# Attention scores and reads of a batch in one call each, by heads of one parity

## The chip, the cores and the metric

The kernel runs on 1 core of one Trainium2 chip. The metric is device time in microseconds of one execution. Its engines are TensorE (PE in the profile, with PEld for its weight loads), VectorE (DVE), ScalarE (ACT), GpSimd (POOL) and SyncE (SP, which issues all DMAs here). They have a queue each and meet only through semaphores.

## The reference, cut to what matters

Attention between x, 8 batches of 8 heads of 512 tokens of 64 values, and a state of 32 rows of 64 values a head, in both directions; then two gated feed-forward layers.

```python
B, H, S, D = x.shape                      # 8, 8, 512, 64; state has Ns = 32 rows a head
scale = 1.0 / np.sqrt(D)
scores = scale * np.matmul(x, state.transpose(0, 1, 3, 2))
scores = scores - scores.max(-1, keepdims=True)
a = np.exp(scores)
a /= a.sum(-1, keepdims=True) + 1e-09
xread = np.matmul(a, state)
scores2 = scale * np.matmul(state, x.transpose(0, 1, 3, 2))
...
sread = np.matmul(a2, x)                  # a2: softmax of scores2 over the tokens
...
x = x @ w_a * (x @ w_b) @ w_out           # first layer, on the 4096 + 256 rows
x = silu(x @ w_gate) * (x @ w_val) @ w_out   # second layer
```

## The kernel before, in words

A block is the 512 tokens of a batch; a ninth block, "s", holds the 256 rows of sread. The first layer runs in steps of f, 128 of the 1536 hidden columns: two products `p` (line 644) into two PSUM banks, their elementwise product `a`, a split of it into a high and a low part `hs`, and four products `po` (line 679) with the output weights. A product is three matmuls, high by high, high by low and low by high, 0.227 us each. The first layer's input weights are first multiplied with the states (`sw`, lines 452 and 453, from `state_w`), so that xread itself is never made: the weights `a` of the attention go straight into the products `p` as `xs`. `sw` is copied out of PSUM (`swo`), goes to DRAM, and comes back as `swr`, split into `swh` and `swl`; that of the first step goes straight into `swr`, eight DMAs of 32 rows. The second layer (from about 710 us on) is made of other lines and isn't touched.

The attention of a batch is two quads g of four heads each. `quad` (lines 483 to 517) loads two pairs of heads of x, transposed (`xt`, 64 values of the even head over 64 of the odd one, 512 tokens). Two matmuls make the scores `psc` (line 493): the weights are a pair's states, 64 columns with zeros where a head doesn't meet its own values, so that a pair fills 64 of the bank's 128 partitions. Batches 0 and 1 (`BY_ROWS`) also make scores with the tokens on the partitions, `pr` (line 509), eight matmuls a quad whose weights are 128 tokens of x. `softmax1` turns scores into `xs`; `softmax2` takes the softmax over the tokens, turns it by four transpositions (`pa`), reads `psr` with x by tokens (`xn`, line 607: eight matmuls of 64 columns of weights and 128 moved columns, half of them a head's values by the other head's weights), scales the result (`sr`, line 613), transposes it (`pst`, line 618) and keeps its valid halves by two copies into `sread` (line 628). All this is in float32, where one matmul of the code is two records in the trace.

The order of the work on each engine is written out by a planner, `Program.order`: it keeps a list of tasks with a due time (`by`), an earliest time (`start`), estimated costs, and numbers of buffers (`ROOM`), and hands each free engine the most urgent task. Copies go to ACT or DVE as it finds them free. Only the order reaches the chip. Two PSUM banks, "pt", serve the scores from batch 1 on, the transpositions, the reads and `sw`. Until the first product, spare matmuls `warm` (line 1043) fill PE.

Of the kernel before, what the change touches and what calls it, by code (L numbers as in the profile page):

```python
# [14 lines left out]
AF = mybir.ActivationFunctionType  # L15
# [3 lines left out]
P = 128  # L19
B, H, S, NS, D = 8, 8, 512, 32, 64  # L20
# [4 lines left out]
NPAIR = H // 2  # L25
# [42 lines left out]
PASS_US, HALF_PASS_US = 0.2267, 0.12  # L68
SWITCH_US = 0.2
# [6 lines left out]
def act(n):  # L76
    return {"ACT": ACT_US[0] + ACT_US[1] * n}
# [181 lines left out]
class Kernel:  # L259
# [183 lines left out]
    def state_w(self, st, fp, p, w, q, by):  # L443

        hi, lo = st
        for h in range(2):
            head = 2 * p + h
            c = slice(head * P, (head + 1) * P)
            ps = self.bank(f"sw{q}_{fp}_{head}")

            def fn(pe, ps=ps, h=h, c=c):
                pe.matmul(ps.t, lhsT=hi.t[:, c], rhs=w.t[:, h], start=True, stop=False)  # L452
                pe.matmul(ps.t, lhsT=lo.t[:, c], rhs=w.t[:, h], start=False, stop=True)  # L453

            self.pe(2 * PASS_US, fn, [hi, lo, (w, (h, 0)), (w, (h, 1))], [ps], by=by)
            r = 32 * (head % 4)
            self.sw_out(
                ps, self.sw_d[q, fp], lambda t, head=head, r=r: t[:, head // 4, r:r + 32].rearrange("b n c -> n b c"), f"swo{q}_{fp}_{head}", by,
                (self.sw_first, head) if q == fp == 0 else None
            )  # L460

# [13 lines left out]

    def attention(self, b, start, span, by_x, by_s):

        raw_st = self.load(
            self.h_buf(f"strt{b}"), self.st_t[b], P * 1024, lambda t: t[:, :NPAIR * 2 * NS], start=start
        )  # L480
        return [self.quad(b, g, start + span * g / 2, span, raw_st, by_x, by_s) for g in range(2)]

    def quad(self, b, g, t0, span, raw_st, by_x, by_s):

        nm = f"{b}_{g}"
        x = [self.load(self.h_buf(f"xt{nm}_{j}"), self.xt[b, 2 * g + j], start=t0) for j in range(2)]
        sT = self.h_buf(f"sT{nm}")
        ps = self.bank(f"psc{nm}", g if b == 0 else None)
        cols = [slice((2 * g + j) * 64, (2 * g + j + 1) * 64) for j in range(2)]

        def fn(pe):
            for j in range(2):
                pe.matmul(
                    ps.t[64 * j:64 * j + 64], lhsT=raw_st.t[:, cols[j]], rhs=x[j].t, start=True, stop=True
                )

        due = t0 + span * 0.15 if b >= BY_ROWS else by_s - 60
        self.pe(4 * PASS_US + SWITCH_US, fn, [raw_st, *x], [ps], by=due)
        self.copy(lambda: sT.t, lambda: ps.t, 512, [ps], [sT], by=due + 2)
        if b >= BY_ROWS:  # L500
            x_hl = self.softmax1(b, g, sT, by_x)
        else:
            pr = self.ring(f"ab{g}", 1, f"pr{nm}", self.ps) if b == 0 else self.bank(f"pr{nm}")

            def by_rows(pe):
                for c in range(4):
                    r = slice(c * P, (c + 1) * P)
                    for j in range(2):
# [59 lines left out]
    def softmax2(self, b, g, sT, by):  # L568

        nc = self.nc  # L570
        nm = f"{b}_{g}"
        e2 = self.h_buf(f"e2{nm}")
        st = self.ring("s2", 4, f"s2{nm}", shape=(4,))
        kw = {"by": by}

        def first(v):
# [5 lines left out]
            out=e2.t, in_=sT.t, func=AF.Exp, scale=SCALE, bias=st.t[:, 1:2], accum_out=st.t[:, 2:3]  # L582
# [17 lines left out]
        ps = self.bank(f"psr{nm}")  # L600

        def fn(pe):
            for c in range(4):
                for j in range(2):
                    l = slice(c * P + 64 * j, c * P + 64 * j + 64)
                    r = slice(c * 256 + P * j, c * 256 + P * j + P)
                    pe.matmul(  # L607
                        ps.t[64 * j:64 * j + 64, :P], lhsT=a2.t[:, l], rhs=xn.t[:, r], start=c == 0, stop=c == 3
                    )

        self.pe(0.9 + SWITCH_US, fn, [a2, xn], [ps], **kw)
        sr = self.h_buf(f"sr{nm}")
        self.p.add(act(P), lambda e: nc.scalar.activation(
            out=sr.t[:, :P], in_=ps.t[:, :P], func=AF.Copy, scale=st.t[:, 3:4]
        ), [ps, st], [sr], **kw)
        pt = self.bank(f"pst{nm}")
# [4 lines left out]
        for h in range(2):  # L621
            rows = slice(64 * h, 64 * h + 64)

            def kept(rows=rows, h=h):
                return pt.t[rows, :P].rearrange("p (j i n) -> p j i n", j=2, n=NS)[:, :, h]

            self.copy(
                lambda rows=rows: self.sread.t[rows, 2 * g:2 * g + 2, b::B], kept, 64, [pt],
                [(self.sread, (b, g, h))], **kw
            )  # L630
# [534 lines left out]
def laid_out(inputs):  # L1165
    x, state = inputs["x"], inputs["state"]
    arrays = {}
    arrays["xt"] = x.transpose(0, 1, 3, 2).reshape(B, NPAIR, P, S)
    arrays["xn"] = x.reshape(B, 2, 4, 4, P, D).transpose(0, 1, 4, 3, 2, 5).reshape(B, 2, P, 1024)

    sp = state.reshape(B, NPAIR, 2, NS, D)
    st_t = np.zeros((B, 2, D, NPAIR, 2, NS), state.dtype)
    for h in range(2):
        st_t[:, h, :, :, h] = sp[:, :, h].transpose(0, 3, 1, 2)
    arrays["st_t"] = st_t.reshape(B, P, NPAIR * 2 * NS)
# [38 lines left out]
```

## Time and profile before

| | |
|---|---|
| median of 3 runs | 1460.92 us (1459.82 to 1461.51) |
| the profiled execution | 1460.34 us, of which its span 1458.6 |
| PE, DVE, ACT busy | 1441.6, 1026.4, 717.4 us |
| mean granted clock | 0.998 |
| matmul records of scores, reads, scores by rows | 64, 256, 64 |
| DMA | 344.73 MB, 236 GB/s |

The span is that from the first to the last instruction. A busy PE is not one at its peak: records overlap, and the time that a group takes of PE is read from where the next group starts. A granted clock of 1 is 2.4 GHz, one of 0.5 is 1.2 GHz. Idle time of an engine that nobody waits for costs nothing.

### The profile page before, as it was taken

The page shows a single profiled execution, that of the slowest core. Times are in us where ns is not written, and L with a number is a line of the kernel's source. Part 1 is how long each engine was busy: PE and PEld are TensorE (multiplying, and loading weights), DVE is VectorE, ACT ScalarE, POOL GpSimd, SP SyncE. Part 2 cuts the span into 40 slices and gives each one's busy share as a digit, 9 for nine tenths or more (in the row PEclk, how much of TensorE's full clock was granted, in tenths as well). Part 3 has the DMA queues.
Part 4 walks back from the last instruction along what each step waited for, and adds up shares of the span by engine and source line. Part 5 has one row for each costly group of instructions (what it writes and reads, how often), then busy time and mean ns, then how long its engine had stood idle before and what let it go on. Part 6 is the DMA issues. An engine that isn't in the chain of part 4 may idle for free.

```text
span 1458.6 us, 19824 instructions
## 1 busy us (share of the span) xinstructions
PE 1441.6 (99%) x6968; PEld 1189.5 (82%) x6968; DVE 1026.4 (70%) x1750; ACT 717.4 (49%) x1276; POOL 103.7 (7%) x78
## 2 busy tenths in 40 slices
PE   9999899999999999999999999999999999999998
PEld 8677688778888888998888888888888888888887
DVE  7899756875778788877687796655955567554464
ACT  7676745753456465655554553333523354323340
POOL 1202201110011111111010100000000000000000
PEclk9999999999999999999999999999999999999999
DMA  8765754762467575856989796675947668365476
GB/s 300 260 244 177 259 174 145 245 228 80 162 217 258 178 263 217 289 205 221 347 316 329 255 358 264 228 257 174 366 169 269 209 233 320 139 246 204 143 263 242
DMA packets 134420, 344.73 MB, mean 236 GB/s; under 512 B 14000, under 2 KB 16048, under 8 KB 134320
## 3 DMA queue, kind: packets, MB, share of 16 engines
q1 hardware_dynamic: 134320, 343.46, 66.4%
q8 instruction: 55, 0.90, 0.3%
q14 instruction: 45, 0.37, 0.1%
HBM read 246.94 MB, written 95.94 MB: 235 GB/s over the span
## 4 chain that ended last, share of the span: by engine, by line
PE 84%; DMA 3%; DVE 2%; ACT 1%; issue 0%; SPq 0%; DVEq 0%; ACTq 0%
PE pX L772 17%; PE pu L931 15%; PE po L679 15%; PE p L644 14%; PE pC L772 8%; PE pY L772 4%; PE p_s L644 2%; PE po_s L679 1%; PE pvs L644 1%; PE pgs L644 1%; PE pus L986 1%; PE sw L452 1%; DMA swr<-sw 1%; PE psr L607 1%; DMA wt<-wt 1%; PE sw L453 1%
## 5 line engine op out<-in xcount | busy, mean ns | idle before, releaser
L679 PE MATMUL po<-hs,wo 128*128 128x512 f32 x1152 | 287.4, 392 | 0.8 <-DVE hs L338 0.4
L679 PEld LDWEIGHTS po<-hs,wo 128*128 128x128 f32 x1152 | 213.9, 188 | 53.4 <-issue 7.3
L931 PE MATMUL pu<-S,wt 128*128 128x512 f32 x1008 | 242.8, 389 | 0.0
L644 PE MATMUL p<-xs,swh 128*128 128x512 f32 x768 | 239.7, 394 | 1.9 <-DVE a L663 1.2
L931 PEld LDWEIGHTS pu<-S,wt 128*128 128x128 f32 x1008 | 188.9, 188 | 39.0
L772 PE MATMUL pX<-x,w 128*128 128x512 f32 x864 | 219.6, 390 | 0.3 <-ACT t L330 0.3
L772 PEld LDWEIGHTS pX<-x,w 128*128 128x128 f32 x864 | 161.9, 188 | 34.6 <-ACT t L330 1.2
L644 PEld LDWEIGHTS p<-xs,swh 128*128 128x128 f32 x768 | 143.6, 189 | 35.4 <-DVE a L663 2.5
L644 PE MATMUL p<-xs,swl 128*128 128x512 f32 x384 | 150.3, 392 | 0.4 <-DVE swl L338 0.4
L780 DVE TENSOR_TENSOR t<-t,pC 128x512 f32<-128x512 f32 x96 | 65.9, 687 | 106.5 <-ACT t L330 94.3
L663 DVE TENSOR_TENSOR a<-a,p 128x512 f32<-128x512 f32 x96 | 65.8, 685 | 75.6 <-PE p L644 60.3
L330 ACT COPY a<-p 128x512 f32<-128x512 f32 x86 | 50.4, 586 | 98.4 <-PE p L644 97.3
L330 ACT COPY t<-pX 128x512 f32<-128x512 f32 x83 | 48.7, 586 | 99.0 <-PE pX L772 95.1
L345 ACT CAST hs<-a 128x512 fp32r<-128x512 f32 x96 | 59.5, 621 | 68.6 <-DVE a L663 56.1
L644 PEld LDWEIGHTS p<-xs,swl 128*128 128x128 f32 x384 | 72.5, 189 | 16.7 <-DVE swl L338 1.3
L338 DVE TENSOR_TENSOR hs<-a,hs 128x512 fp32r<-128x512 f32 x96 | 67.5, 704 | 14.7 <-ACT hs L345 14.2
L772 PE MATMUL pX<-x,wg 128*128 128x512 f32 x288 | 73.2, 390 | 0.0
L772 PE MATMUL pY<-x,wg 128*128 128x512 f32 x288 | 73.1, 389 | 0.0
L772 PE MATMUL pC<-x,wv 128*128 128x512 f32 x288 | 73.1, 389 | 0.0
L772 PE MATMUL pC<-x,w 128*128 128x512 f32 x288 | 73.1, 389 | 0.0
L338 DVE TENSOR_TENSOR swl<-swr,swh 128x1024 fp32r<-128x1024 f32 x48 | 59.8, 1246 | 11.0 <-ACT swh L345 6.4
L786 ACT ACTIVATE gv<-pX 128x512 f32<-128x512 f32 x48 | 28.7, 598 | 74.2 <-PE pX L772 74.2
(181 smaller groups left out, 2214.1 us busy)
## 6 DMA issues: line engine op xcount, KB each, us to landing
w<-w SPq DMA_DIRECT2D x120, 512.0 KB, 5.7
wt<-wt SPq DMA_DIRECT2D x84, 512.0 KB, 6.6
sw<-swo SPq DMA_DIRECT2D x96, 256.0 KB, 3.2
wg<-w2g SPq DMA_DIRECT2D x48, 512.0 KB, 5.6
swr<-sw SPq DMA_DIRECT2D x47, 512.0 KB, 5.1
raw_w<-in_wab SPq DMA_DIRECT2D x24, 512.0 KB, 6.3
wv<-w2v SPq DMA_DIRECT2D x36, 256.0 KB, 6.9
xt<-in_xt SPq DMA_DIRECT2D x32, 256.0 KB, 5.1
```

The source lines that it names most:

```text
L330: self.nc.scalar.copy(out(), in_())
L338: lambda e: self.by_engine[e].tensor_tensor(out=out(), in0=in0(), in1=in1(), op=ALU.subtract), r, w, **kw
L345: self.p.add(act(n), lambda e: self.nc.scalar.copy(hi(), src()), [src_buf], [hb], **kw)
L452: pe.matmul(ps.t, lhsT=hi.t[:, c], rhs=w.t[:, h], start=True, stop=False)
L453: pe.matmul(ps.t, lhsT=lo.t[:, c], rhs=w.t[:, h], start=False, stop=True)
L644: pe.matmul(ps.t[:, :n], lhsT=l, rhs=r, start=i == 0, stop=i == last)
L663: self.vec(n, lambda v, a=a, pb=pb: v.tensor_tensor(out=a.t[:, :n], in0=a.t[:, :n], in1=pb.t[:, :n], op=ALU.mult), [pb], [a])
L679: pe.matmul(ps.t[:, :n], lhsT=wo[f].t[:, hw, c], rhs=hs.t[:, hh, :n], start=st, stop=sp)
L772: pe.matmul(ps.t, lhsT=w.t[:, half, hw, i * P:(i + 1) * P], rhs=x.t[:, hx], start=start and i == n == 0, stop=stop and i == 1 and n == 2, ...
L780: self.vec(512, lambda e: e.tensor_tensor(out=to(), in0=a(), in1=b(), op=op), r, [w], **kw)
L786: self.p.add(act(n), lambda e: self.nc.scalar.activation(out=out.t[:, :n], in_=ps.t[:, :n], func=AF.Silu), [ps], [out])
L931: pe.matmul(ps.t, lhsT=w.t[:, half, hw, c], rhs=x.t[:, hx], start=starts and k == m == 0, stop=stops and k == n - 1 and m == 2, skip_group ...
```

## The change

Heads are now grouped by parity: bank and softmax h hold the four heads 2j + h of a batch, j from 0 to 3, and the quads are gone. The layout of the states loses its zeros (32 columns a pair), `xn` and the rows of `sw` in DRAM are put in the new order of heads, with DMAs of the same sizes. Scores are one call a batch, eight matmuls with tiles of 64 rows by 32 columns of weights, into two banks. Scores by rows are 32 matmuls a batch of 64x128 tiles and 32 moved columns. The reads are one call a batch, 32 matmuls of 128x32 tiles and 64 moved columns into one bank, with no part left unused; its scaling is two ACT instructions of 64 columns, its transposition one for two, and the copy into `sread` one for four. All four loads of a batch's x have one earliest time, for batches 0 and 1 halfway to their block (`X_LATER`).

```diff
+X_LATER = 0.5
...
-            r = 32 * (head % 4)
+            r = 32 * (head // 2)
...
-                lambda: raw.t[r:r + 32, head // 4], lambda: o.t[::4], [o], [(raw, head)], 32 * 2048, by=by + 3
+                lambda: raw.t[r:r + 32, head % 2], lambda: o.t[::4], [o], [(raw, head)], 32 * 2048, by=by + 3
...
-        return [self.quad(b, g, start + span * g / 2, span, raw_st, by_x, by_s) for g in range(2)]
...
-        x = [self.load(self.h_buf(f"xt{nm}_{j}"), self.xt[b, 2 * g + j], start=t0) for j in range(2)]
...
+        n = NPAIR * NS
+        raw_st = self.load(self.h_buf(f"strt{b}"), self.st_t[b], P * 4 * n, lambda t: t[:, :n], start=start)
+        t0 = start + span * X_LATER if b < BY_ROWS else start
+        xt = [self.load(self.h_buf(f"xt{b}_{j}"), self.xt[b, j], start=t0) for j in range(NPAIR)]
+        heads = [
+            (h, j, slice(D * h, D * h + D), slice(NS * j, NS * j + NS)) for j in range(NPAIR) for h in range(2)
+        ]
...
             def by_rows(pe):
                 for c in range(4):
-                    r = slice(c * P, (c + 1) * P)
-                    for j in range(2):
+                    for h, j, rows, cs in heads:
                         pe.matmul(
-                            pr.t[:, c * P + 64 * j:c * P + 64 * j + 64], lhsT=x[j].t[:, r],
-                            rhs=raw_st.t[:, cols[j]], start=c == j == 0, stop=True, skip_group_check=True
+                            pr[h].t[:, c * P + NS * j:c * P + NS * j + NS], lhsT=xt[j].t[rows, c * P:(c + 1) * P],
+                            rhs=raw_st.t[rows, cs], start=c == j == 0, stop=True, skip_group_check=True
                         )
...
+        psc = [self.bank(f"psc{b}_{h}", h if b == 0 else None) for h in range(2)]
+
+        def scores(pe):
+            for h, j, rows, cs in heads:
+                pe.matmul(psc[h].t[cs], lhsT=raw_st.t[rows, cs], rhs=xt[j].t[rows], start=True, stop=True)
+
+        self.pe(4 * PASS_US + SWITCH_US, scores, [raw_st, *xt], psc, by=due)
...
+            for h, (a2, xn, _) in enumerate(parts):
+                for c in range(4):
+                    for j in range(NPAIR):
+                        rows = slice(NS * j, NS * j + NS)
+                        pe.matmul(
+                            ps.t[rows, h * D:h * D + D], lhsT=a2.t[:, c * P + NS * j:c * P + NS * j + NS],
+                            rhs=xn.t[:, c * 256 + D * j:c * 256 + D * j + D], start=c == 0, stop=c == 3,
+                            skip_group_check=True
+                        )
+
+        self.pe(1.1 + SWITCH_US, fn, [t for a2, xn, _ in parts for t in (a2, xn)], [ps], **kw)
+        sr = self.h_buf(f"sr{b}")
+        for h, (_, _, st) in enumerate(parts):
+            c = slice(h * D, h * D + D)
+            self.p.add(act(D), lambda e, c=c, st=st: nc.scalar.activation(
+                out=sr.t[:, c], in_=ps.t[:, c], func=AF.Copy, scale=st.t[:, 3:4]
+            ), [ps, st], [(sr, h)], **kw)
...
+        self.copy(
+            lambda: self.sread.t[:, :, b::B], lambda: pt.t[:, :P].rearrange("p (j n) -> p j n", j=NPAIR), P, [pt],
+            [(self.sread, b)], **kw
+        )
```

The planner's order changes nearly everywhere. Three places matter below. The first is SP's queue at the end of the start: `swr0_0` is the input of the first product, `xt1_...` are the loads of batch 1's x. Before:

```order
L319 DMA swr0_0_293<-swo0_0_5_343 32x512
L319 DMA sw0_0_300<-swo0_0_4_332 32x4x512
L319 DMA swr0_0_293<-swo0_0_6_353 32x512
L319 DMA xt1_1_0_376<-in_xt 128x512
L319 DMA xt1_1_1_385<-in_xt 128x512
L319 DMA swr0_0_293<-swo0_0_7_362 32x512
L319 DMA sw0_0_300<-swo0_0_5_343 32x4x512
L319 DMA sw0_0_300<-swo0_0_6_353 32x4x512
L319 DMA sw0_0_300<-swo0_0_7_362 32x4x512
```

Now, at the same place of SP's queue:

```order
L320 DMA swr0_0_289<-swo0_0_6_350 32x512
L320 DMA swr0_0_289<-swo0_0_7_356 32x512
L320 DMA sw0_0_303<-swo0_0_5_331 32x4x512
L320 DMA sw0_0_303<-swo0_0_6_350 32x4x512
L320 DMA xt1_0_393<-in_xt 128x512
L320 DMA xt1_1_398<-in_xt 128x512
L320 DMA xt1_2_404<-in_xt 128x512
L320 DMA xt1_3_411<-in_xt 128x512
L320 DMA sw0_0_303<-swo0_0_7_356 32x4x512
```

The four loads of batch 1 stand behind the last `swr0_0`; before, two stood ahead of it and the other two were issued earlier still.

The second is PE just ahead of `p0_1_0_0`, the first product of block 1; `sw1_0_...` are products of weights and states for the batches 4 to 7, `pat` the transpositions in softmax1. Before:

```order
L452 MATMUL sw1_0_5_569<-w1_0_2_238,st1_hi_324 128x512
L453 MATMUL sw1_0_5_569<-w1_0_2_238,st1_lo_370 128x512
L1043 MATMUL warm_76<-ident_65 128x128 x2
L452 MATMUL sw1_0_6_588<-w1_0_3_251,st1_hi_324 128x512
L453 MATMUL sw1_0_6_588<-w1_0_3_251,st1_lo_370 128x512
L644 MATMUL p0_1_0_0_593<-xs1_0_429,swh1_0_502 128x512 x2
```

Now, on PE just ahead of the same product:

```order
L454 MATMUL sw1_0_7_602<-w1_0_3_250,st1_lo_376 128x512
L559 MATMUL pat1_0_609<-ident_65,sn1_0_550 128x128 x4
L559 MATMUL pat1_1_618<-ident_65,sn1_1_554 128x128 x4
L506 MATMUL psc1_0_636<-xt1_0_393,strt1_116 32x512
L506 MATMUL psc1_1_637<-xt1_0_393,strt1_116 32x512
L506 MATMUL psc1_0_636<-xt1_1_398,strt1_116 32x512
L506 MATMUL psc1_1_637<-xt1_1_398,strt1_116 32x512
L506 MATMUL psc1_0_636<-xt1_2_404,strt1_116 32x512
L506 MATMUL psc1_1_637<-xt1_2_404,strt1_116 32x512
L506 MATMUL psc1_0_636<-xt1_3_411,strt1_116 32x512
L506 MATMUL psc1_1_637<-xt1_3_411,strt1_116 32x512
L646 MATMUL p0_1_0_0_648<-xs1_0_623,swh1_0_536 128x512 x2
```

Both transpositions of batch 1 and its scores now stand there, and the eighth `sw1_0`, which before came later.

The third is PE at the reads of batch 2, in block 0. Before:

```order
L452 MATMUL sw1_3_5_2088<-w1_3_2_1639,st1_hi_324 128x512
L453 MATMUL sw1_3_5_2088<-w1_3_2_1639,st1_lo_370 128x512
L607 MATMUL psr2_0_2096<-xn2_0_1850,a22_0_2073 64x128 x8
L607 MATMUL psr2_1_2108<-xn2_1_1873,a22_1_2077 64x128 x8
L679 MATMUL po0_0_2_1939<-hs0_0_6_1970,wo1_6_1967 128x512 x3
L618 MATMUL pst2_0_2124<-ident_65,sr2_0_2117 128x128
L618 MATMUL pst2_1_2126<-ident_65,sr2_1_2122 128x128
L679 MATMUL po0_0_3_1951<-hs0_0_6_1970,wo1_6_1967 128x512 x3
```

Now, on PE at the same reads:

```order
L681 MATMUL po0_0_0_1956<-hs0_0_6_2052,wo1_6_2010 128x512 x3
L681 MATMUL po0_0_1_1968<-hs0_0_6_2052,wo1_6_2010 128x512 x3
L612 MATMUL psr2_2164<-xn2_0_1930,a22_0_2135 32x64 x16
L612 MATMUL psr2_2164<-xn2_1_1954,a22_1_2137 32x64 x16
L681 MATMUL po0_0_2_1980<-hs0_0_6_2052,wo1_6_2010 128x512 x3
L453 MATMUL sw1_3_6_2204<-w1_3_3_1678,st1_hi_341 128x512
L454 MATMUL sw1_3_6_2204<-w1_3_3_1678,st1_lo_376 128x512
L627 MATMUL pst2_2207<-ident_65,sr2_2201 128x128
L681 MATMUL po0_0_3_1998<-hs0_0_6_2052,wo1_6_2010 128x512 x3
```

Two calls of eight matmuls are one call of 32, and two transpositions are one, with another pair of `sw` between.

## Rows read from the trace of the kernel before

**Rows 1.** The page, part 1: busy us (share of the span) and instructions of each engine
```profile
PE 1441.6 (99%) x6968; PEld 1189.5 (82%) x6968; DVE 1026.4 (70%) x1750; ACT 717.4 (49%) x1276; POOL 103.7 (7%) x78
```

**Rows 2.** Stretches: us; busy us (x) of PE, PEld, DVE, ACT, POOL; PEclk; DMA share, GB/s
```profile
52.90:170.00 117.10, 113.32 (x535) 85.40 (x534) 107.48 (x192) 83.63 (x153) 21.68 (x14) 1.00 0.66 231
170.00:310.00 140.00, 135.28 (x632) 107.14 (x631) 98.98 (x162) 84.19 (x146) 21.27 (x14) 0.99 0.58 200
310.00:600.00 290.00, 290.00 (x1392) 234.07 (x1391) 219.31 (x398) 153.27 (x269) 24.50 (x18) 1.00 0.56 201
```

**Rows 3.** What PE waited for: us in total, times, longest us
```profile
PE sw L452 <- ACT swo L330: 5.8, 7, 3.2
```

**Rows 4.** A stretch behind the longest of those waits, columns as in rows 2
```profile
181.00:185.00 4.00, 4.00 (x12) 3.16 (x11) 1.29 (x2) 1.83 (x3) 0.00 (x0) 0.60 0.70 261
```

**Rows 5.** Timeline of PE, scores: start us, us, instruction, records, idle before
```profile
62.92 1.08 PE L493 MATMUL psc<-xt,strt 128*64 128x512 f32 x4
63.93 0.97 PE L679 MATMUL po<-hs,wo 128*128 128x512 f32 x3
```

**Rows 6.** The same scores, 63.25 to 63.35 us only
```profile
62.92 0.65 PE L493 MATMUL psc<-xt,strt 128*64 128x512 f32 x2
```

**Rows 7.** The same scores, 63.65 to 63.8 us only
```profile
63.40 0.60 PE L493 MATMUL psc<-xt,strt 128*64 128x512 f32 x2
```

**Rows 8.** Scores (L493) by stretch: us; busy us (records) of PE, PEld; PEclk; DMA
```profile
52.90:170.00 117.10, 5.40 (x20) 0.99 (x20) 1.00 0.66 231
170.00:600.00 430.00, 8.64 (x32) 1.58 (x32) 1.00 0.57 201
```

**Rows 9.** Timeline of PE, reads of batch 7
```profile
586.53 1.97 PE L607 MATMUL psr<-xn,a 128*64 128x128 f32 x32
588.43 0.73 PE L644 MATMUL p<-xs,swh 128*128 128x512 f32 x2
...
589.92 0.38 PE L618 MATMUL pst<-ident,sr 128*128 128x128 f32 x2
590.06 0.70 PE L644 MATMUL p<-xs,swh 128*128 128x512 f32 x2
```

**Rows 10.** Last reads of batch 0, 127.96 to 127.98 us only
```profile
127.78 0.28 PE L607 MATMUL psr<-xn,a 128*64 128x128 f32 x2
```

**Rows 11.** Reads (L607) by stretch, columns as in rows 8
```profile
52.90:170.00 117.10, 3.94 (x64) 3.45 (x64) 1.00 0.66 231
170.00:600.00 430.00, 11.81 (x192) 10.36 (x192) 1.00 0.57 201
```

**Rows 12.** Timeline of PE, scores by rows, and first products of blocks 0 and 1
```profile
37.46 1.90 PE L509 MATMUL pr<-strt,xt 128*128 128x64 f32 x16
39.17 0.71 PE L644 MATMUL p<-xs,swh 128*128 128x512 f32 x2
...
52.90 0.63 PE L644 MATMUL p<-xs,swh 128*128 128x512 f32 x2
```

**Rows 13.** Timeline of SP's queue before the first product
```profile
32.58 2.02 SPq L319 DMA_DIRECT2D xt<-in_xt  x2
34.70 0.47 SPq L319 DMA_DIRECT2D swr<-swo  x1
```

**Rows 14.** Timeline of ACT before the first product
```profile
7.00 0.67 ACT L375 ACTIVATE cv_w<-raw_w 128x512 f32<-128x512 f32 x1 [4.99 <-DMA raw_w<-in_wab]
...
37.88 1.04 ACT L345 CAST swh<-swr 128x1024 fp32r<-128x1024 f32 x1 [1.89 <-DMA sw<-swo]
38.84 0.58 ACT L330 COPY swo<-sw 128x512 f32<-128x512 f32 x1
```

**Rows 15.** Timeline of DVE, two steps of the softmax
```profile
28.40 1.28 DVE L551 TENSOR_TENSOR sn<-sn,sm 128x512 f32<-128x512 f32 x2
```

**Rows 16.** Instructions that touch sread: ns min/median/max, first and last start
```profile
L332 DVE COPY sread<-pst x20: 223/282/303, 133.9 to 590.9; 64x64 f32<-64x64 f32 x20
```

More of the change, by code (lines that the diff above doesn't have):

```diff
@@ new lines, in attention @@
+        n = NPAIR * NS
[5 more added lines that the diff above has]
+        ]
+        pr = []
+        if b < BY_ROWS:
+            pr = [
+                self.ring(f"ab{h}", 1, f"pr{b}_{h}", self.ps) if b == 0 else self.bank(f"pr{b}_{h}") for h in range(2)
+            ]
@@ L505, in by_rows @@
             def by_rows(pe):
                 for c in range(4):
-                    r = slice(c * P, (c + 1) * P)
-                    for j in range(2):
+                    for h, j, rows, cs in heads:
                         pe.matmul(
-                            pr.t[:, c * P + 64 * j:c * P + 64 * j + 64], lhsT=x[j].t[:, r],
-                            rhs=raw_st.t[:, cols[j]], start=c == j == 0, stop=True, skip_group_check=True
-                        )
-            self.pe(8 * PASS_US, by_rows, [raw_st, *x], [pr], by=t0 + span * 0.15)
@@ L515, in quad @@
-            x_hl = self.softmax1(b, g, pr, by_x)
-        self.softmax2(b, g, sT, by_s)
-        return x_hl
+                            pr[h].t[:, c * P + NS * j:c * P + NS * j + NS], lhsT=xt[j].t[rows, c * P:(c + 1) * P],
+                            rhs=raw_st.t[rows, cs], start=c == j == 0, stop=True, skip_group_check=True
+                        )
+            self.pe(3.6 + SWITCH_US, by_rows, [raw_st, *xt], pr, by=start + span * 0.15)
+        due = start + span * 0.15 if b >= BY_ROWS else by_s - 60
@@ new lines, in attention @@
+        psc = [self.bank(f"psc{b}_{h}", h if b == 0 else None) for h in range(2)]
[3 more added lines that the diff above has]
+        self.pe(4 * PASS_US + SWITCH_US, scores, [raw_st, *xt], psc, by=due)
+        out, parts = [], []
+        for h in range(2):
+            sT = self.h_buf(f"sT{b}_{h}")
+            self.copy(lambda sT=sT: sT.t, lambda h=h: psc[h].t, 512, [psc[h]], [sT], by=due + 2)
+            out.append(self.softmax1(b, h, pr[h] if pr else sT, by_x))
+            parts.append(self.softmax2(b, h, sT, by_s))
@@ L519, in softmax1 @@
+        self.reads(b, parts, by_s)
+        return out
     def softmax1(self, b, g, scores, by):
@@ L599, in softmax2, with reads @@
         self.copy(lambda: a2.t, lambda: pa.t, 512, [pa], [a2], **kw)
-        ps = self.bank(f"psr{nm}")
-        def fn(pe):
[L603 to L616, printed above, removed]
+        return a2, xn, st
+    def reads(self, b, parts, by):
+        nc = self.nc
+        kw = {"by": by}
+        ps = self.bank(f"psr{b}")
+        def fn(pe):
+            for h, (a2, xn, _) in enumerate(parts):
[14 more added lines that the diff above has]
+            ), [ps, st], [(sr, h)], **kw)
+        pt = self.bank(f"pst{b}")
         self.pe(
@@ L619, in softmax2 @@
         )
[L621 to L630, printed above, removed]
+        self.copy(
+            lambda: self.sread.t[:, :, b::B], lambda: pt.t[:, :P].rearrange("p (j n) -> p j n", j=NPAIR), P, [pt],
+            [(self.sread, b)], **kw
+        )
     def main(self, us, fn, r, w):
@@ L1168, in laid_out @@
     arrays["xt"] = x.transpose(0, 1, 3, 2).reshape(B, NPAIR, P, S)
-    arrays["xn"] = x.reshape(B, 2, 4, 4, P, D).transpose(0, 1, 4, 3, 2, 5).reshape(B, 2, P, 1024)
+    arrays["xn"] = x.reshape(B, NPAIR, 2, 4, P, D).transpose(0, 2, 4, 3, 1, 5).reshape(B, 2, P, 1024)
     sp = state.reshape(B, NPAIR, 2, NS, D)
[L1172 to L1175, printed above, removed]
+    arrays["st_t"] = sp.transpose(0, 2, 4, 1, 3).reshape(B, P, NPAIR * NS)
     st_1 = np.zeros((2, 2, D, H, NS, 4), state.dtype)
```

23 lines of the change are left out of this document (2 added, 21 removed).

## The prediction

> **What bounds the kernel now.** Read first the busy shares: PE is busy for 1441.6 of 1458.6 us, DVE for 70% [rows 1]. Busy is not the same as useful, so the next view is that of stretches [rows 2]: from 310 to 600 us PE has no idle moment in 290 us, while DVE has 219 and ACT 153. There every us that leaves PE leaves the kernel. From 52.9 to 170 us it is otherwise: PE is busy for 113.3 of 117.1 us, but DVE for 107.5, 92%, so that two engines are nearly full, and what PE saves there may come back as a wait for DVE. The third view is what PE waits for [rows 3]: the largest item is a product of the weights with the states (sw) that waits for ACT's copy of an earlier one, since both go through the two banks "pt": 5.8 us in 7 waits, the longest 3.2. Behind that one the granted clock was 0.60 for 4 us, and PE got 12 products done, which at 0.227 us each are 2.7 us of work [rows 4]. So waits are small in sum, one of them is dear, and the kernel is bound by PE's own work from about 53 us on; before that by a chain through ACT, DVE and DMA. I call slot the time from the first matmul of a group to the first of what follows.
>
> **The change part by part.** Scores first. A call has two matmuls of 128x64 tiles in two records each; its slot is 63.93 - 62.92 = 1.01 us [rows 5]. Between 63.25 and 63.35 us two records are in flight, started together, and between 63.65 and 63.8 us the other two [rows 6, 7]: two column tiles move at once, and a slot is two passes of 0.48 us. There are 20 records, 5 calls, between 52.9 and 170 us, and 32, 8 calls, behind it [rows 8]. The change makes one call of eight tiles a batch. If all eight move at once its slot is 1.01 again, plus some starts: I take 1.05. If the two halves of rows take turns, it has four passes: 1.9. If only two tiles ever move at once, eight passes: 3.9. No row shows row tiles, so these are the bounds; nearest is the row on column tiles, which move together, so 1.05. Behind 52.9 us six calls remain, those of batches 2 to 7 (batch 1's stands ahead of block 1's first product in the new order): two in the first stretch, 5 x 1.01 - 2 x 1.05 = 2.95 us less, and four behind it, 8 x 1.01 - 4 x 1.05 = 3.9 less.
>
> Reads. Two quads back to back have 32 records and a slot of 588.43 - 586.53 = 1.90 us [rows 9]; here too two end together [rows 10], so that is 16 rounds of 0.109 and 0.16 at the ends. The new call has 64 records, in four tiles at once again 16 rounds, each of 64 columns for 128. Bounds: half a round, 16 x 0.0545 + 0.16 = 1.03, or no gain from fewer columns, 1.90. I take 1.03, since the scores' passes of 0.48 us for 512 columns and the reads' 0.109 for 128 stand nearly as their columns do. That is 0.87 less a batch: 64 records, two batches, in the first stretch, 1.74 us, and six behind it, 5.2 [rows 11]. One transposition of the result a batch goes, a slot of 590.06 - 589.92 = 0.14 [rows 9]: 0.3 and 0.85.
> The Trainium skill speaks against this step: TensorEngine Tiling (Array Packing), section Performance Considerations, says that each matmul has some 60 cycles of overhead, that one of a single column takes as long as one of 60, and that a tiling factor should not be taken from a dimension that is already small. Here 64 columns are left. By it the reads would fall under rival three; the two records that end together speak against a toll that is paid one by one, but no row has 64 columns in such a tile.
>
> Scores by rows. Before, 16 records of 128x128 weights and 64 columns have a slot of 39.17 - 37.46 = 1.71 [rows 12]; two calls, 3.4 us a batch. After, 64 records on two row tiles: 32 rounds of the same 0.107, 3.4, if both halves load their weights at once, 6.8 if not. I take 3.4. Batch 0's lies in the start, where warm-up matmuls fill PE; batch 1's now stands behind block 0's first two products, not before them.
>
> The start. In the old queue of SP two loads of batch 1's x are issued just ahead of the last swr: 2.1 us until that one goes out [rows 13], and ACT then waits 1.89 us for it before swh and the first product, at 39.17 [rows 14, 12]. The new queue has four of these loads, but behind all of swr: up to 2.1 us earlier. ACT also has less ahead of swh, since batch 1's softmax has moved: one copy of scores, one Exp, one cast and two copies of sw, about 0.5 us each (a copy is 0.58 long [rows 14] and neighbours overlap a little): 2.5. And raw_w now goes ahead of x, where ACT's first work waited for it until 7.00: 0 to 2. So block 0's first product comes 4.6 to 6.7 us earlier. But between it and block 1's (13.7 us later before, [rows 12]) now stand two products of block 0 (12 x 0.227 = 2.7), the scores by rows (3.4) and the softmax of both heads: ten steps of DVE of 0.6 us [rows 15], 0.8 for the small ones, an Exp, transpositions, split and hops some 2.5, together 9.3, so 15.4. Left at block 1's first product: 2.9 to 5.0. I take 4; bounds 0 (all of it lost to the loads of x) and 6. That product also has one more sw of the states ahead of it (sw1_0_7, four passes less a half: 0.45 us), which the next stretch then lacks.
>
> The sum. First stretch, PE: 2.95 + 1.74 + 0.3 + 0.45 = 5.4 us less. DVE is the cover that may be gone: of its own work the copies into sread go, 8 of 0.28 [rows 16] against 2 of about 0.33, 1.6 us, shared with ACT. So the stretch gives between 1.6 and 5.4; I take the middle, 3.5. Second stretch: 3.9 + 5.2 + 0.85 = 9.95, full since PE doesn't idle. With 4 of the start: 17.45. The profiled execution took 1460.3 (1458.6 of span and 1.7 around it), 0.6 under the median of 1460.92, so the forecast is 1443.4, said as 1443. The wait of 3.2 us and its slow clock may go or come again elsewhere: 4 us either way, kept for the range.
>
> **The rivals.** One, row tiles take turns: the slot of scores is 1.9 (+0.85 x 6 = 5.1) and the by-rows call of batch 1 costs 3.4 more on the path: +8.5, 1452. For it: no row has two row tiles. Against: column tiles overlap.
> In a sentence apart: the Trainium skill, TensorE: Matmul & The Clock Gate, Part 3, has sixteen tiles of 32x32 at 10.6 times one, and by that this rival would fall; no row here shows it.
> Two, the time falls to DVE: 92% busy between 52.9 and 170 us, with a batch's two heads now asked for together and one call of scores needing both pt banks at once. Then start and first stretch give nothing and only the 9.95 stays: 1451.
> Three, a record of 64 columns costs what one of 128 does: the reads keep 1.90, +0.87 x 8 = 7: 1450. The rule of the Trainium skill's page TensorEngine Tiling (Array Packing) told above is of this kind.
> Four, slower: no more than two tiles move at once, as in all rows here. Scores then have a slot of 3.9 (+2.85 x 6 = 17.1) and the reads keep 1.90 (+7): 1467. It decides, past 1463.8, once a call of scores costs over 3.3 us (20.4 - 7 = 13.4 over six). This is also the case in which the change doesn't do what it says.
>
> **How the numbers follow.** Below 0.2%, 2.9 us, a measurement of this kernel can't tell a change from none. Forecast 0.57 (its own range 1437 to 1449, from 0 to 6 of the start, 1.6 to 5.4 of the stretch and the chance wait); one 0.14; two 0.12; three 0.08; four 0.05; two of the first three together, 1456 to 1460, 0.04. All but four, the upper half of the last and some of two are faster: 0.90; no change 0.05; slower 0.05. The range for 8 in 10 goes from 1437 to 1453, where one, two and three still lie.
>
> **What would show it.** One call of scores a batch, eight matmuls with a slot near 1.05: 1.9 says rival one, 3.9 rival four. Reads in a slot near 1.03: 1.9 says rival three. Batch 1's scores by rows near 3.4 between two products of block 0. Block 1's first product near 49 us for 52.90. Then the first stretch: if PE's waits there grow by more than 2 us, it is rival two. From 310 us on no idle PE, and per batch about 2 us less. The forecast is wrong if a new wait of over 5 us stands before 310 us.

## The result and the profile after

The changed kernel takes 1436.05 us (median of 4 runs, 1435.3 to 1438.12) beside 1460.7 for the kernel before in the same comparison: a ratio of 0.9834, 95% interval 0.9817 to 0.9851. That is 24.7 us less. The forecast was 1443, 17.5 us less, with a range from 1437 to 1453: the direction is right, the size is not, and the time lies 1 us below the range. The profiled execution has a span of 1433.5 us for 1458.6, 25.1 less.

The page of the changed kernel, part 1, as in [rows 1]:

```profile
PE 1421.5 (99%) x7344; PEld 1182.4 (82%) x7344; DVE 1015.3 (71%) x1726; ACT 718.2 (50%) x1276; POOL 101.6 (7%) x78
```

The same three stretches as in [rows 2]:

```profile
52.90:170.00 117.10, 115.38 (x659) 90.81 (x659) 109.10 (x197) 89.78 (x164) 21.11 (x16) 0.99 0.70 239
170.00:310.00 140.00, 139.11 (x746) 112.00 (x745) 105.94 (x173) 87.49 (x150) 18.63 (x13) 1.00 0.62 217
310.00:600.00 290.00, 290.00 (x1660) 240.90 (x1659) 219.70 (x399) 160.32 (x285) 27.06 (x21) 1.00 0.60 213
```

In each of the first two PE is idle for less than before: 1.7 and 0.9 us against 3.8 and 4.7 [rows 2]. What PE waits for between 57.3 and 310 us (us in total, times, longest), in the kernel before, the four dearest of seven items:

```profile
PE sw L452 <- ACT swo L330: 5.0, 6, 3.2
PE p L644 <- DVE a L663: 1.2, 2, 0.9
PE p L644 <- ACT a L330: 0.6, 1, 0.6
PE po L679 <- DVE hs L338: 0.4, 1, 0.4
```

and in the changed kernel, all of them:

```profile
PE sw L453 <- ACT swo L331: 1.2, 4, 0.5
PE pst L627 <- ACT sr L622: 0.8, 2, 0.7
```

The wait of 3.2 us of [rows 3] is gone, and so are most of the small ones. Over the whole span sw still waits 5.2 us for swo, but 4.0 of them lie in the start, where something else went wrong.

**Scores, reads and scores by rows.** Timeline of PE in the changed kernel, the scores of one batch; the second piece is the view cut to 67.69 to 67.72 us:

```profile
67.69 1.09 PE L506 MATMUL psc<-xt,strt 64*32 64x512 f32 x16
68.71 0.96 PE L681 MATMUL po<-hs,wo 128*128 128x512 f32 x3
```

```profile
67.69 0.64 PE L506 MATMUL psc<-xt,strt 64*32 64x512 f32 x5
```

Eight tiles in two records each have a slot of 1.02 us, as two column tiles had [rows 5], and within 0.03 us five records are in flight. The last reads, the transposition behind them, and the scores by rows of batch 1:

```profile
564.63 1.10 PE L612 MATMUL psr<-xn,a 128*32 128x64 f32 x64
565.66 0.73 PE L646 MATMUL p<-xs,swh 128*128 128x512 f32 x2
...
567.15 0.27 PE L627 MATMUL pst<-ident,sr 128*128 128x128 f32 x1
```

```profile
39.23 3.76 PE L495 MATMUL pr<-strt,xt 64*128 64x32 f32 x64
42.92 0.73 PE L646 MATMUL p<-xs,swh 128*128 128x512 f32 x2
```

Reads take 1.03 where they took 1.90 [rows 9], scores by rows 3.69.

**The start.** PE in the changed kernel from block 0's first product to block 1's:

```profile
36.42 0.62 PE L646 MATMUL p<-xs,swh 128*128 128x512 f32 x2
...
46.46 0.39 PE L454 MATMUL sw<-w,st_lo 128*128 128x512 f32 x1
46.69 2.39 PE L1045 MATMUL warm<-ident 128*128 128x128 f32 x20
51.06 0.50 PE L453 MATMUL sw<-w,st_hi 128*128 128x512 f32 x1 [1.98 <-ACT swo L331]
...
51.74 0.63 PE L453 MATMUL sw<-w,st_hi 128*128 128x512 f32 x1
52.17 0.63 PE L454 MATMUL sw<-w,st_lo 128*128 128x512 f32 x1
52.68 1.97 PE L559 MATMUL pat<-ident,sn 128*128 128x128 f32 x8
55.19 1.94 PE L506 MATMUL psc<-xt,strt 64*32 64x512 f32 x16 [0.55 <-DVE xs L339]
57.06 0.73 PE L646 MATMUL p<-xs,swh 128*128 128x512 f32 x2
```

Block 0 begins 2.7 us earlier than in [rows 12], block 1 4.2 us later. ACT, DVE and SP's queue in the same place:

```profile
45.41 1.06 ACT L346 CAST swh<-swr 128x1024 fp32r<-128x1024 f32 x1 [2.99 <-DMA swr<-sw]
46.36 0.58 ACT L331 COPY a<-p 128x512 f32<-128x512 f32 x1
46.84 0.62 ACT L423 CAST w<-cv_w 64x512 fp32r<-64x512 f32 x1
47.36 1.15 ACT L539 ACTIVATE sn<-sn 128x512 f32<-128x512 f32 x2
48.53 1.87 ACT L423 CAST w<-cv_w 64x512 fp32r<-64x512 f32 x3
50.42 1.07 ACT L331 COPY swo<-sw 128x512 f32<-128x512 f32 x2
```

```profile
44.23 1.28 DVE L535 TENSOR_TENSOR sn<-pr,mx 128x512 f32<-128x512 f32 x2
```

```profile
36.66 2.96 SPq L320 DMA_DIRECT2D sw<-swo  x4
39.88 0.39 SPq L320 DMA_DIRECT2D swr<-sw  x1
```

ACT does its work in the order written. It stands 2.99 us at a cast of swr, whose load SP issued at 39.88, and block 1's Exp and the copies of sw stand behind it: the Exp's input is ready from DVE at 45.5, and the Exp begins at 47.36. PE has only spare matmuls, then nothing for 1.98 us. Then the clock falls, and is back at 1.00 by 55 us (stretches, columns as in [rows 2]):

```profile
50.00:54.00 4.00, 2.94 (x10) 2.06 (x11) 2.32 (x4) 2.82 (x6) 1.28 (x1) 0.68 0.40 148
52.00:54.00 2.00, 2.00 (x8) 1.31 (x8) 0.32 (x1) 1.34 (x3) 1.15 (x1) 0.50 0.79 296
55.00:58.00 3.00, 2.81 (x20) 1.12 (x21) 2.75 (x5) 2.20 (x5) 0.00 (x0) 1.00 0.80 253
```

A matmul of sw at 0.50 takes 0.43 us (51.74 to 52.17) for 0.227. The scores call behind it has a slot of 1.87 us (55.19 to 57.06), nearly twice 1.02, but by then the clock is at 1.00. The call needs both banks of "pt", and each still holds a head's transpositions until DVE has made `xs` of them. PE with the view cut to 55.1 to 56.0 us, and DVE:

```profile
55.19 1.04 PE L506 MATMUL psc<-xt,strt 64*32 64x512 f32 x2 [0.55 <-DVE xs L339]
```

```profile
55.30 0.69 DVE L339 TENSOR_TENSOR xs<-pat,xs 128x512 fp32r<-128x512 f32 x1 [0.16 <-ACT xs L346]
```

Two of the 16 records begin before 56.0 us, the other 14 later: DVE is done with the second bank at 55.99.

**Where 25.1 us come from.** I add up PE's records from block 1's first product on. "Own work" is the time of scores, reads and the reads' transpositions, from start to the start of what follows. "Stall" is, over all matmuls of p, po and sw followed by another of these, the time from start to start above 0.2267 us (24 of them take 5.44 us where nothing disturbs them); it holds waits, the slow clock behind a wait, and stoppages too short to show as idle. Differences are taken before rounding.

| | before | after | difference |
| --- | --- | --- | --- |
| block 1's first product, us | 52.9 | 57.1 | +4.2 |
| own work | 29.5 | 14.7 | -14.9 |
| stall | 20.2 | 6.9 | -13.4 |
| the rest | | | -1.0 |

### The profile page after: what moved, and what is told of

It reads as the page before. It is cut to its first block, busy times and chain, and to the rows that moved or that the text cites. A ratio compares the mean times of both kernels' runs of the same rounds, so it can differ in the third digit from the quotient of the medians.

```text
span 1433.5 us, 20548 instructions
## 1 busy us (share of the span) xinstructions
PE 1421.5 (99%) x7344; PEld 1182.4 (82%) x7344; DVE 1015.3 (71%) x1726; ACT 718.2 (50%) x1276; POOL 101.6 (7%) x78
## 4 chain that ended last, share of the span: by engine, by line
PE 93%; DVE 1%; ACT 1%; issue 0%; ACTq 0%; DVEq 0%
PE pX L774 18%; PE po L681 18%; PE p L646 17%; PE pu L933 16%; PE pC L774 9%; PE pY L774 5%; PE p_s L646 2%; PE po_s L681 1%; PE pvs L646 1%; PE pgs L646 1%; PE sw L453 1%; PE pus L988 1%; PE sw L454 1%; ACT w L423 1%; PE pa L593 0%; PE psr L612 0%
## 5 line engine op out<-in xcount | busy, mean ns | idle before, releaser
L681 PE MATMUL po<-hs,wo 128*128 128x512 f32 x1152 | 283.2, 391 | 0.0
L646 PEld LDWEIGHTS p<-xs,swl 128*128 128x128 f32 x384 | 72.1, 188 | 15.3
L339 DVE TENSOR_TENSOR swl<-swr,swh 128x1024 fp32r<-128x1024 f32 x48 | 59.8, 1246 | 10.5 <-PE p L646 4.7
```

Source lines behind the costliest of these rows:

```text
L339: lambda e: self.by_engine[e].tensor_tensor(out=out(), in0=in0(), in1=in1(), op=ALU.subtract), r, w, **kw
L646: pe.matmul(ps.t[:, :n], lhsT=l, rhs=r, start=i == 0, stop=i == last)
L681: pe.matmul(ps.t[:, :n], lhsT=wo[f].t[:, hw, c], rhs=hs.t[:, hh, :n], start=st, stop=sp)
```

## The experiments

Two theories on the 13.4 us. A: the change takes tasks and uses of the two banks out of a batch (from batch 2 on six uses of a bank where there were eight, one copy into sread where there were four), and what waits in the crowded stretch up to 310 us waits less. B: the planner writes another order for every kernel, and that of before had bad luck, that of after good luck. "Stall" below is that of the profiled execution.

| kernel | us | ratio to before [95%] | block 1 at | own | stall |
| --- | --- | --- | --- | --- | --- |
| pad | 1448.39 | 0.9928 [0.9906, 0.9949] | 63.0 | 26.9 | 6.3 |
| light | 1455.83 | 0.9973 [0.9960, 0.9986] | 53.5 | 21.4 | 22.1 |
| b_hop | 1456.43 | 0.9987 [0.9974, 0.9999] | 53.7 | 29.6 | 15.2 |
| a_hop | 1434.61 | 0.9828 [0.9806, 0.9850] | 54.9 | 14.6 | 9.5 |
| b_later | 1455.18 | 0.9965 [0.9954, 0.9977] | 51.9 | 30.4 | 14.4 |
| a_early | 1438.08 | 0.9853 [0.9838, 0.9867] | 53.0 | 15.7 | 11.5 |
| a_two | 1440.33 | 0.9867 [0.9852, 0.9882] | 57.3 | 16.3 | 8.6 |
| a_tail | 1441.79 | 0.9876 [0.9859, 0.9892] | 57.9 | 15.8 | 12.7 |
| a_both | 1444.27 | 0.9895 [0.9875, 0.9915] | 59.1 | 17.0 | 14.0 |
| a_copies | 1437.74 | 0.9851 [0.9834, 0.9868] | 57.0 | 15.3 | 10.4 |
| a_bank | 1439.63 | 0.9864 [0.9845, 0.9884] | 56.8 | 16.2 | 10.6 |
| a_start | 1434.60 | 0.9829 [0.9811, 0.9848] | 54.0 | 15.7 | 8.8 |
| b_hop2 | 1459.43 | 0.9997 [0.9977, 1.0017] | 53.1 | 29.7 | 17.3 |
| a_hop2 | 1443.75 | 0.9892 [0.9864, 0.9921] | 58.5 | 14.6 | 14.0 |
| b_dma | 1455.37 | 0.9969 [0.9955, 0.9984] | 55.7 | 31.6 | 12.6 |
| a_dma | 1437.82 | 0.9852 [0.9823, 0.9880] | 56.0 | 15.7 | 9.7 |
| after_again | 1436.86 | 0.9845 [0.9827, 0.9863] | 58.2 | 14.7 | 7.4 |
| a_best | 1435.41 | 0.9841 [0.9824, 0.9858] | 55.2 | 14.6 | 9.2 |

**Is it PE's work?** pad does scores and reads of the changed kernel twice, in the same order; light leaves three quarters of the reads out of the kernel before (c = 1 to 3), in the same order.

```diff
 pad
+            for _ in range(2):
                 for h, j, rows, cs in heads:
                     pe.matmul(psc[h].t[cs], ...
-            for h, (a2, xn, _) in enumerate(parts):
+            for h, (a2, xn, _) in [(h, p) for _ in range(2) for h, p in enumerate(parts)]:
 light
-            for c in range(4):
+            for c in range(1):
```

> The changed kernel with PE's saved work given back and nothing else: each call of scores and of reads is done twice, with the planner's costs as they were, so that the order of all other work is the same. Scores again cost 0.87 us more a call (two more passes of 0.43), the reads 0.90. If each us of PE counts from block 1 on: 7 x 0.87 + 8 x 0.90 = 13.3, so 1449. If PE has slack between 57 and 170 us (DVE full), the two reads and two or three scores there cost nothing: 1445. If the gain were all PE work, with nothing from fewer waits, it should come near the 1460 of before.

> The kernel before, in its own order, with three quarters of the reads left out (the terms c = 1 to 3 of a2 times x are not computed): 12 of 16 rounds of 0.109 us a batch, 1.31 x 8 = 10.5 us of PE work less. If PE work counts in full everywhere: 1450. If the stretch from 53 to 170 us is DVE's, the two batches there give nothing: 1453. If waits take the place of the work, over 1455.

pad has 12.2 us more of own work than the changed kernel and takes 12.4 more by the medians, 13.7 by the ratios; its stalls are no larger. The two numbers don't measure quite the same: in pad's profiled execution, 3.2 us above its median, block 1 begins 6.0 us later (PE stood still for 3.83 us, and the doubled scores call behind it met a clock of 0.50), and from there to the end it takes 1386.8 us for 1376.5. So 10.3 of the 12.2 us come through, and the changed kernel is bound by PE from block 1 on. light takes 8.1 us of own work out of the kernel before and gains 3.6 by the median. PE's waits in light between 57.3 and 310 us:

```profile
PE sw L452 <- ACT swo L330: 5.2, 5, 3.1
PE p L644 <- ACT a L330: 3.3, 2, 2.7
PE pst L618 <- ACT sr L613: 1.9, 2, 1.5
```

They grow where before had 5.0, 0.6 and 0.2. So less work on PE alone doesn't remove the stalls, and in the kernel before a part of it comes back as waits for ACT.

**Is it the order?** The planner's two hand-over times, and then its time of a transfer, are changed in both kernels: no instruction is added or taken.

```diff
-HOP_US, PE_HOP_US = 0.25, 0.3
+HOP_US, PE_HOP_US = 0.27, 0.32          b_hop, a_hop
+HOP_US, PE_HOP_US = 0.23, 0.28          b_hop2, a_hop2
-DMA_US, ... = 2.2, ...
+DMA_US, ... = 2.4, ...                  b_dma, a_dma
```

> The kernel before with the planner's two constants for a hop between engines raised by 0.02 us, which changes no work, only the order. Theory order: the 12 us that PE loses by waits behind 52.9 us are chance of one order, so another one differs by several us, 1448 to 1470. Theory structure: they belong to two quads a batch (more calls through the pt banks, more copies), so any order has them: 1458 to 1464.

> The changed kernel with the same two constants raised by 0.02 us. Theory order: the changed kernel's few waits were luck, another order has some of the 9 us back: 1438 to 1448. Theory structure: within 3 us of 1436.

> The kernel before with the planner's two hand-over times set to 0.23 and 0.28 us: the same instructions in another order. If the change itself removes the stalls, TensorE's stalls behind block 1's first product stay at 14 to 21 us here; if the order of before was bad luck, they can come out at 7 to 12, and the time falls to 1446 to 1452 us.

> The changed kernel with the same two constants, 0.23 and 0.28 us. If the change itself removes the stalls, they are 7 to 12 us and the time is 1433 to 1440 us; if its order was good luck, they come out at 14 us or more, and the time at 1441 us or above.

> The kernel before with the planner's time of a transfer at 2.4 us instead of 2.2: another order again. If the change removes the stalls, they stay at 14 to 21 us and the time at 1454 to 1462 us; if it is luck, below 12 us and under 1452.

> The changed kernel with the same constant, 2.4 us. If the change removes the stalls, they are 7 to 12 us and the time is 1432 to 1440 us; if it is luck, 14 us or more and 1441 us or above. One of block 1's two Exp stands ahead of ScalarE's cast that waited 2.99 us, so block 1's first product may start 1 to 3 us earlier than 57.1.

The three pairs give differences of 21.8, 15.7 and 17.6 us; the two kernels as they are give 24.7. Stalls fall by 5.7, 3.3 and 2.9 in the pairs, by 13.4 in the kernels as they are. So both theories hold in part, and neither of the two clean outcomes I had named came: a_hop2 has 14.0 us of stalls, more than b_dma's 12.6. The waits alone, as the view of PE's waits sums them between 57 and 310 us, lie further apart: 8.1 us in the kernel before, 8.3, 7.4 and 6.0 in b_hop, b_hop2 and b_dma, but 2.0 in the changed kernel and 3.1, 4.9 and 3.7 in a_hop, a_hop2 and a_dma. The waits of a_hop2 between 57.3 and 310 us show it is the same kind of wait that came back:

```profile
PE sw L453 <- ACT swo L331: 2.5, 4, 1.2
PE sw L453 <- DVE swo L333: 1.3, 4, 0.4
```

With the constants of the pairs the change is worth 18.4 us on the mean; by these three draws some 6 of the 24.7 are how the two orders fell out.

**Is it the loads of the start?** b_later loads batches 0 and 1 of the kernel before at the later time of the changed kernel; a_early does the reverse.

```diff
 b_later
-        return [self.quad(b, g, start + span * g / 2, span, ...) for g in range(2)]
+        at = [start + span * (g / 2 if b >= BY_ROWS else 0.5) for g in range(2)]
+        return [self.quad(b, g, at[g], span, ...) for g in range(2)]
 a_early
-X_LATER = 0.5
+X_LATER = 0.0
```

> The kernel before with one thing of the change: all four loads of x of batches 0 and 1 have their earliest time halfway to the block, as X_LATER does. Theory later: a later block 1 gives ACT and DVE a lead, and the 9 us of waits on PE behind it go: 1448 to 1453, with block 1's first product past 55 us. Theory calls: the waits belong to two scores, two reads and four copies a batch: 1456 to 1462.

> The changed kernel with X_LATER at 0 instead of 0.5, so that batch 1's x may be loaded from the beginning. Theory later: block 1's first product comes some 4 us earlier than 57 and the waits behind it come back: 1436 to 1442. Theory calls: it comes earlier and the waits stay low: 1431 to 1434.

Neither carries the gain. b_later doesn't try theory later, since block 1 begins at 51.9 us in it and not past 55; it is 4.8 us faster than before, no more than another order is (b_dma: 5.0). a_early comes out as theory later had it: block 1 begins 4.1 us earlier than in the changed kernel, the stalls behind it are 4.6 larger, and the time is 1438.08, though 2.0 us more is less than can be told. So a part of the lower stalls may be the other side of the late start. It can't be all: a_hop2 starts block 1 at 58.5 and has 14.0 us of stalls.

**Is it banks and small steps?** a_two makes two calls of the scores, one for each bank. a_tail gives each parity its own read call, scaling, transposition and two copies, so that a batch uses eight banks as before; a_copies has its four copies alone, a_bank its two banks with a copy each, a_both is a_two and a_tail.

```diff
 a_two
-        self.pe(4 * PASS_US + SWITCH_US, scores, [raw_st, *xt], psc, by=due)
         for h in range(2):
+            self.pe(4 * PASS_US + SWITCH_US, scores, [raw_st, *xt], [psc[h]], by=due)
 a_tail, a_bank
-        ps = self.bank(f"psr{b}")
+        for h, (a2, xn, st) in enumerate(parts):
+            ps = self.bank(f"psr{b}_{h}")
...
+            pt = self.bank(f"pst{b}_{h}")
 a_tail, a_copies
-        self.copy(lambda: self.sread.t[:, :, b::B], ...
+            for g in range(2):
+                self.copy(lambda rows=rows, g=g: self.sread.t[rows, 2 * g:2 * g + 2, b::B], ...
```

> The changed kernel with the scores of a batch in two calls, one for each parity and bank, of four 64x32 tiles. If only PE's slot counts: 1.02 + 0.1 more a call, seven calls on the path, +7.8: 1444. If the second call also brings waits back: 1447 or more. If four tiles of one row half pass in less than 1.02 us: under 1442.

> The changed kernel with the tail of the reads as it was before in number: for each parity a call of its own (16 matmuls of 128x32 tiles), a scaling of 128 columns, a transposition, and two copies of 64x64 into sread; eight pt banks a batch where the change has six. PE: 0.17 for the split call, 0.1 for its entry and 0.14 for the transposition, 0.4 x 8 = 3.3: 1439. If banks and small copies are what makes PE wait, 3 to 8 us more: 1442 to 1447.

> The changed kernel with the scores in two calls (one for each parity and bank) and with one read call, scaling, transposition and two 64x64 copies for each parity, so eight banks of the pool a batch as the kernel before had. Beside the changed kernel's 1436.0 us the scores alone cost 4.3 us and the reads' tail 5.7 us. If the costs are work of TensorE and a few steps each, they add: 1446 us, with under 4 us of TensorE's waits between 57 and 310 us. If it is the number of banks and of small steps in a batch that made the waits of the kernel before, the waits come back: over 6 us between 57 and 310 us, and 1449 to 1453 us. If the two kernels' orders of instructions differ by luck, the waits stay as low as in the changed kernel (2 us) and the time is 1442 to 1446 us.

> The changed kernel with the one copy of the reads into their place split into four of 64x64, as before: three small instructions more a batch on VectorE or ScalarE, some 0.28 us each in the trace, nothing more on TensorE. If the small copies hold a bank of the pool and so delay TensorE, the time rises by 1.5 to 3 us (1437.5 to 1439), with waits of TensorE above 2 us between 57 and 310 us; if the engines beside TensorE have room for them, it stays within 1 us of 1436.

> The changed kernel with a read call, a scaling, a transposition and one copy for each parity: eight banks a batch instead of six, two copies a batch instead of one. TensorE's work grows by about 0.4 us a batch, 3.3 us in all. If that work and nothing else was the cost of the split tail, 1439.3 us; if the two banks more a batch cost waits as well, 1441 to 1442 us as with the four copies; if the copies were the cost, 1436 to 1438.

a_two costs 4.3 us and only 1.7 of stalls. That the two calls often stand back to back and then share a slot, I had not expected (timeline of PE):

```profile
64.24 1.19 PE L509 MATMUL psc<-xt,strt 64*32 64x512 f32 x16
65.36 1.65 PE L682 MATMUL po<-hs,wo 128*128 128x512 f32 x6
```

Both calls together take 1.12 us here, and 1.02 in five of the seven batches behind block 1's first product. a_tail costs 5.7 us, with 5.8 more of stalls; a_copies and a_bank 1.7 and 3.6, with 3.6 and 3.7. The costs of a_two and a_tail don't quite add (8.2 in a_both for 4.3 + 5.7), and a_both's stalls of 14.0 stand among those of the five orders of before (12.6 to 20.2). The row of steps is as theory A wants it: 6.9 (six banks, one copy), 10.4 and 10.6, 12.7, 14.0. But a plain other order moved the changed kernel's stall by 2.7 to 7.2 us, so no single one of these steps is told from the draw, and a_copies is slower by less than can be told. All five came out slower, and with more stalls, 11.3 us on the mean; but so large are the stalls in every other order of the changed kernel too (a_hop, a_hop2, a_dma, a_early, a_start and a_best: 8.8 to 14.0, mean 10.5), so this says little for theory A. Nor do the waits of the kernel before come back with eight banks and four copies: between 57 and 310 us they are 5.1 us in a_tail and 4.3 in a_both, where over 6 had been named, for 6.0 to 8.3 in the four orders of before above. What in the change lowers the waits is not shown. The hold of a bank by itself wasn't tried: there is no bank to add.

**The late start.** a_start doubles the size that the planner takes for one load, swr of block 1, which moves ACT's cast of it behind the two Exp; the load is the same. a_best adds the hand-over times of a_hop to it, beside the changed kernel again.

```diff
-            ... [d], [raw], P * 4096, start=start
+            ... [d], [raw], P * 4096 * (2 if (b, fp) == (1, 0) else 1), start=start
```

> The changed kernel with the planner's size of one load doubled (the products for block 1's first pair of steps, swr of batch 1), which puts ScalarE's cast of it behind block 1's two Exp instead of ahead of them; the load itself is unchanged. If ScalarE's wait of 2.99 us for that load is what made block 1 start 4.2 us late, block 1's first product starts at 52 to 54.5 us instead of 57.1 and the time falls to 1432 to 1434.5 us. If the late start comes from the three waits on ScalarE's copies of the products for the second pair and from the lower granted clock around 50 us, the start moves by under 1.5 us and the time stays at 1435 to 1437.

> The changed kernel unaltered, as the measure for the next one on the same chip: 1436 us.

> The changed kernel with the planner's size of block 1's first load of products doubled and its two hand-over times at 0.27 and 0.32 us: the same instructions in an order in which ScalarE casts that load behind block 1's Exp, and in which a hand-over is planned as the run of the other order had it. If the start's gain of some 3 us reaches the end, 1431 to 1433.5 us. If TensorE gives it back in stalls between 57 and 310 us, as it did in part when the load's size alone was changed, or if the order is just another draw, 1434 to 1438 us.

ACT and PE in a_start, and the granted clock in the place where it had fallen:

```profile
46.53 1.15 ACT L539 ACTIVATE sn<-sn 128x512 f32<-128x512 f32 x2
47.59 1.03 ACT L346 CAST swh<-swr 128x1024 fp32r<-128x1024 f32 x1
```

```profile
53.45 0.50 PE L453 MATMUL sw<-w,st_hi 128*128 128x512 f32 x1 [0.74 <-DVE xs L339]
...
54.01 0.62 PE L646 MATMUL p<-xs,swh 128*128 128x512 f32 x2
```

```profile
50.00:54.00 4.00, 2.77 (x16) 1.84 (x15) 4.00 (x6) 3.05 (x6) 1.07 (x1) 1.00 0.55 203
54.00:58.00 4.00, 4.00 (x19) 3.30 (x18) 3.81 (x7) 2.67 (x5) 0.21 (x1) 1.00 0.91 234
```

The wait of 2.99 us is gone, PE's longest stop ahead of block 1 is 0.74, the clock stays at 1.00 (2.4 GHz), and block 1 begins 3.1 us earlier, as foretold, though block 0 had begun 1.2 us later in this execution, since the clock was 0.50 between 12 and 18 us. But the edit moved more than the cast: batch 1's scores call, 1.87 us ahead of block 1 in the changed kernel, comes behind block 1's first product here. The 3.1 us are not the cast's alone. 2.1 of them are given back by block 0's step 8 (268.8 us for 269.8), chiefly in 1.8 us more of stalls and in the scores call, which takes 1.02 us there. The time, 1434.60, is 1.4 us lower and just misses the 1432 to 1434.5 foretold; a_best beside after_again is 1.5 lower, as foretold for a gain that is given back. The intervals overlap in both cases, so none of these kernels beats the changed one by more than can be told.

## Why the prediction was off

**Right: scores, reads, transpositions.** The forecast took 6.85 + 6.94 + 1.15 = 14.9 us from them, behind block 1's first product; the records give 14.9. Slots were 1.02 and 1.03 for 1.05 and 1.03 foretold, by rows 3.69 for 3.4. With that rivals one, three and four fall: the row tiles of the scores don't take turns, and in the reads 64 columns cost half of 128.
Beside it: the overhead of some 60 cycles a matmul that the Trainium skill, TensorEngine Tiling (Array Packing), Performance Considerations, gives doesn't show in the reads; 60 cycles at 2.4 GHz would be 25 ns, an estimate from that page, and 64 records of 64 columns in 1.03 us are 16 ns each, with four tiles in the array. The measurement decides. The prediction had read this rule as a sign for rival three; but the Trainium skill has a single column take as long as 60 there, and the reads' 64 columns lie above that.

**Wrong, the larger part: "the stretch gives between 1.6 and 5.4; I take the middle, 3.5", and the second stretch "full since PE doesn't idle".** The first product of block 0's step 4 stands at 168.75 before and at 160.10 after; from a start 4.2 us late that is 12.8 us gained in the first stretch. The second, from there to the second layer's first product (716.93 and 692.69), gained 15.6 for 9.95. The step took PE's stalls as given and asked only whether DVE would eat the gain. But [rows 2] showed 3.8 and 4.7 us of idle PE in the two stretches, and "PE doesn't idle" is true from 310 us on only. I had seen the wait of 3.2 us and its slow clock and put it down as chance, "4 us either way"; it went, and so did some 9 us of smaller stalls. Of the 13.4, the three pairs give 3 to 6 to the change; the rest is how the two orders fell out and in part, perhaps, the late start. The runs don't part it more finely, and which part of the change lowers the waits stays open.

**Wrong, with the other sign: "I take 4" for the start.** Block 0's first product came 2.7 us earlier (4.6 to 6.7 foretold), but block 1's 4.2 later, 8.2 off and beyond the bound of 0. The step added up the chain of the softmax, 15.4 us, with an Exp at its place, and didn't ask what stands ahead of the Exp in ACT's queue: a cast that waits 2.99 us for a load that SP issues behind four writes. It also left out the clock, which was 0.50 from 52 to 54 us behind PE's stop of 1.98. And it put batch 1's scores call at nothing: the sum takes that call out of the first stretch, since it now stands ahead of block 1's first product, but the 15.4 us up to that product hold no term for it. It cost a stop of 0.55 us and a slot of 1.87, 0.85 of it a wait for the second bank. From block 0's first product to block 1's it took 20.6 us where the sum has 15.4 + 0.45. How these causes share the 8.2 us is not shown: a_start removed ACT's wait, the fall of the clock and the call together, and its block 1 still began at 54.0, 5 us behind the foretold 49.

**The balance.** Forecast: -14.9 - 0.45 - 4 + 1.9 (kept back for DVE) = -17.45. Measured: -14.9 + 4.2 - 13.4 - 1.0 = -25.1. Two errors of 8 and 15 us with opposite signs left 7.7, and they may hang together: in a_early and a_start the start came 4.1 and 3.1 us earlier, and stalls were 4.6 and 1.9 larger. That the mean over the four pairs of orders is 19.9 us, near the 17.5 foretold, would be luck: neither term was right.

**Rival two** (the time falls to DVE) fell: DVE is busy for 109.1 of 117.1 us in the first stretch, more than before, and PE's waits there fell.

## What to carry to other kernels

Where an order is planned from estimates, any edit draws a new order: here that moved the time by 1 to 8 us with no change of work. Measure a few orders of both kernels (a constant nudged) before a gain of that size is put down to the edit, and give a forecast that width. Read idle time in a stretch as something an edit can win as well as lose, above all where a small pool of buffers is shared. For a chain that is moved, write down the queue of each engine it passes and find the entry ahead of it that waits for something else; and give a price to every call that now stands on the chain, also to one whose price was taken off elsewhere.

## What the runs showed of the hardware

- Eight fp32 tiles of 64x32, 512 columns each, take 1.02 us, as two tiles of 128x64 did [rows 5]. Two calls of four tiles each, with nothing between them, share their time as well: in a_two 1.02 us for both in five batches, 1.12 and 1.33 in two.
- Behind 1.98 us in which PE stood still, the granted clock was 0.50 (1.2 GHz) from 52 to 54 us, and a matmul of sw took 0.43 us for 0.227; in a_hop, behind a stop of 1.76 us at the same place, and in a_start, where the longest was 0.74, the clock stayed at 1.00.
- 64 records of 64x128 weights with 32 columns in two row tiles took 3.69 us, 58 ns each, where 32 of 128x128 with 64 columns took 3.4 [rows 12]: halving the columns and doubling the tiles gained nothing there.
